# A linear-attention and dense kernel: the second block's loads go behind the boot's feature transfers, and some DMAs change their queue

## The chip, the cores and the metric

The kernel runs on one core of one Trainium2 chip. The time is that of the device in microseconds (us) for one execution. Before the change it is 690.11 us, the median of three runs (689.63 to 690.3).

The core has five engines that run side by side, each in the order of its own instructions: TensorE (PE: matmuls, and PEld: the loading of their weights), VectorE (DVE), ScalarE (ACT), GpSimd (POOL) and SyncE (SP, which only issues DMAs here). ScalarE and GpSimd issue DMAs too, each on a queue of its own.

## What is computed

```python
# r, k, v, w: (B, H, S, D) = (4, 8, 768, 48); u: (H, D)
for t in range(S):
    cur = einsum('bhd,bhe->bhde', u[None] * k[t], v[t])
    y[:, :, t] = einsum('bhd,bhde->bhe', r[t], state + cur)
    state = w[t][..., None] * state + einsum('bhd,bhe->bhde', k[t], v[t])
x = y.transpose(0, 2, 1, 3).reshape(3072, 384)
h = x @ w_in                    # w_in (384, 2048)
out = (h - tanh(h)) @ w_out     # w_out (2048, 384)
```

## The kernel before

**Blocks.** The 3072 tokens are eight blocks of 384 (two for each of the four sequences). For each block an attention part makes the features `xT` (384 features by 384 tokens), and a dense part takes them through 16 slices of 128 hidden units (`NF` = 16; the loop variable is `f`). While the dense part of block i runs, the attention of block i+1 is worked in between its steps. Only block 0 has its attention alone in front; this is called the boot.

**Attention of a block.** Inputs are the tiles `kq` (keys), `rp` (receptances), `wt` (decays), `v_sb`, and `rmix` and `kmix`, copies of r and k in which every second token is multiplied by `u` (the "mix"). Scores inside chunks of 64 tokens are built in levels m = 1, 2, 4, ... 32. Level 1 multiplies `kmix` and `rmix` on TensorE (`gram`, L219 to L237) and copies the wanted scores under a mask (L242). The later levels use `kq` and `rp` and after each of them both are multiplied by decays (`decay`, L267); products of decays come from `totals` (L253). After level 32 comes `turn` (transposes of `kq`, L317), `update` (matmuls at L335, states on VectorE at L345) and `result` (matmuls at L364 and L382, copies on ScalarE at L395 into `xT`, and into `late` for the last pair of heads). `late` is moved into the free rows of `xT` by six small DMAs (`fill_holes`, L402). These are the feature transfers, or fills; all six are issued by SyncE.

**Dense step f.** `first` makes three matmul pairs into `hp` (L476), six ScalarE activations (`h`, `s`, `qa`, `qb`, `th`, `big`, L483 to L488) and hands back five VectorE operations (L493 to L501) which are issued one step later. `Second.add` multiplies the slice by `w_out` into three accumulators (L514), three steps later (`LAG`); with the last slice ScalarE copies each accumulator to a tile `o` (L518) and issues its DMA to the output (L520).

**Weights.** They arrive as 16 tiles of 768 KB (`raw`) in a ring of three buffers. Each is turned into fp32 by two ScalarE activations (L165, L166) and three VectorE operations (L168, L169, L171). The first three loads are issued by SyncE, the others by GpSimd as buffers come free. Six tiles are converted in the boot, the other ten during block 0's dense steps 0 to 9 (their VectorE part one step later).

**Order.** Inside `manual_schedule(engines=...)` the named engines keep the order in which the program is written; the others are ordered by a scheduler with a cost model. In the boot only TensorE keeps the written order; in the loop TensorE, VectorE and ScalarE do. SyncE's DMA issues are placed by the scheduler everywhere. `plan(i)` says at which step f of block i's dense part each phase of block i+1's attention is put (`phases`), and at which step each preparation for a block is (`prep`: loads; `kmix`, `rmix`, the multiplication by `u`, L435; `totals`; `kq` and `rp`, the first decays). For i = 0 the levels start at step 3, otherwise at step 0. Input tiles have one buffer each, so a load for block i+2 waits until block i+1 has read the tile for the last time.

Of the kernel before, what the change touches and what calls it, by code (L numbers as in the profile page):

```python
# [37 lines left out]
F32 = mybir.dt.float32  # L38
# [4 lines left out]
AF = mybir.ActivationFunctionType  # L43
ALU = mybir.AluOpType
PSUM = bass.MemoryType.PSUM
PE, DVE, ACT = (getattr(mybir.EngineType, n) for n in ("PE", "DVE", "Activation"))

B, H, S, D = 4, 8, 768, 48
P = 128
# [12 lines left out]
NF = FF // P  # L62
N = B * S
# [20 lines left out]
def kernel(  # L84
# [10 lines left out]
    nc = tc.nc  # L95

    const = ctx.enter_context(tc.tile_pool(name="const", bufs=1))
# [10 lines left out]
    shift = const.tile([P, 3], F32, name="shift", tag="shift")  # L108
    for i, value in enumerate((QUAD[0][0], QUAD[1][0], -SMALL)):
        nc.vector.memset(shift[:, i:i + 1], value)  # L110
    u_sb = const.tile([P, NPAIR], F32, name="u_sb", tag="u_sb")
    nc.sync.dma_start(out=u_sb, in_=uT)

# [41 lines left out]
    def load_weights(f, queue):  # L155
        raw = conv.tile([P, 2 * DM, 2], I32, name="raw", tag="raw")
        queue.dma_start(out=raw, in_=weights[f].bitcast(I32).rearrange("p (n two) -> p n two", two=2))
        return f, raw

    def convert(f, raw):  # L160

        lo, hi = raw[:, :, 0], raw[:, :, 1]
        a = w_sb[:, f, :].bitcast(I32)
        up = conv.tile([P, 2 * DM], I32, name="up", tag="up", bufs=2)
        nc.scalar.activation(out=a.bitcast(F32), in_=hi.bitcast(F32), func=AF.Copy, scale=HIGH_SCALE)  # L165
        nc.scalar.activation(out=up, in_=lo.bitcast(U32), func=AF.Copy, scale=2.0 ** -29)  # L166
        return [
            lambda: nc.vector.tensor_single_scalar(a, a, 3, op=ALU.logical_shift_left),  # L168
            lambda: nc.vector.scalar_tensor_tensor(out=a, in0=hi, scalar=-2 ** 31, in1=a,  # L169
                                                   op0=ALU.bitwise_and, op1=ALU.bitwise_or),  # L170
            lambda: nc.vector.tensor_tensor(out=a, in0=a, in1=up, op=ALU.add)]  # L171
# [7 lines left out]
    class Block:  # L179
# [266 lines left out]
        def start(self, ps):  # L446

            for p0 in HALVES:
                for name, src in (("kq", kT), ("rp", rT), ("wt", wT)):
                    self.load(name, src, p0, UP)  # L450
            for name in ("rmix", "kmix"):
                self.tiles[name] = inp.tile([P, NPAIR * NB], F32, name=name, tag=name)
            yield
            for p0 in HALVES:
                self.mix(p0, UP)
                self.level_1(ps, p0)
                self.decay(1, p0, UP)
                self.totals(1, p0, UP)
            for m in (2, 4, 8, 16, 32):
                for p0 in HALVES:  # L460
                    self.level(ps, m, p0, UP)
                    self.totals(m, p0, UP)
            for p0 in HALVES:
                self.turn(ps, p0)
                self.update(ps, p0)
            for p0 in HALVES:
                self.result(ps, list(range(p0, p0 + UP)), p0 != HALVES[0])
                if p0 == HALVES[0]:
                    self.fill_holes([nc.sync])
            yield  # L470


# [30 lines left out]
    class Second:  # L503
# [5 lines left out]
        def add(self, f, g):  # L509
            if f == 0:  # L510
                self.acc = [self.ps.tile([P, DM], F32, name=f"acc{j}", tag=f"acc{j}", bufs=1)
                            for j in range(NB // P)]
            for j, acc in enumerate(self.acc):
                nc.tensor.matmul(acc, lhsT=g[:, j * P:(j + 1) * P], rhs=w_out_sb[:, f, :],  # L514
                                 start=(f == 0), stop=(f == NF - 1))
                if f == NF - 1:
                    o = dense.tile([P, DM], F32, name="o", tag="o")
                    nc.scalar.activation(out=o, in_=acc, func=AF.Copy, scale=1.0 / UPSCALE)  # L518
                    r0 = self.row0 + j * P
                    nc.scalar.dma_start(out=out[r0:r0 + P, :], in_=o)  # L520

    def plan(i):

        names = ("level 1", 2, 4, 8, 16, 32, "turn", "update")
        first_step = 3 if i == 0 else 0
        phases = {first_step + n: name for n, name in enumerate(names)}
        result = first_step + len(names) + 1
        phases[result] = "result"
        prep = {}

        def put(f, block, *what):
            prep.setdefault(f, []).extend((block, name) for name in what)

        if i == 0:
            put(0, 1, "kmix", "rmix")
            put(1, 1, "totals 1", "kq")
            put(2, 1, "totals 2", "rp")
        put(first_step + 1, i + 2, "load 1")
        put(first_step + 7, i + 2, "load 2")
        put(result + 1, i + 2, "load 3")  # L540
        for f, name in zip(range(NF - 6, NF), ("kmix", "rmix", "totals 1", "totals 2", "kq", "rp")):
            put(f, i + 2, name)
        return phases, prep

    blocks = [Block(b, q) for b in range(B) for q in range(NQ)]
    with tc.manual_schedule(engines={PE}), \
            tc.tile_pool(name="ps_boot", bufs=4, space=PSUM) as boot:
        xT = blocks[0].begin()
        start = blocks[0].start(boot)
        next(start)  # L550
        raws = [load_weights(0, nc.sync)]
        blocks[0].load_v()
        for f in range(1, RAWS):
            raws.append(load_weights(f, nc.sync))
        next(start)
        for f in range(AHEAD):
            for op in convert(*raws.pop(0)):
                op()
            raws.append(load_weights(f + RAWS, nc.gpsimd))
        for name in ("load 1", "load 2"):  # L560
            blocks[1].prepare(name)
    ps_d = ctx.enter_context(tc.tile_pool(name="ps_d", bufs=1, space=PSUM))
    ps_a = ctx.enter_context(tc.tile_pool(name="ps_a", bufs=2, space=PSUM))
    with tc.manual_schedule(engines={PE, DVE, ACT}):
        blocks[1].prepare("load 3")
        waiting, rest, extra = [], [], []
        for i, blk in enumerate(blocks):
            here = xT
            later = blocks[i + 1] if i + 1 < len(blocks) else None
            if later:  # L570
                xT = later.begin()
            phases, preparations = plan(i)
            second = Second(blk.b * S + blk.q * NB, ps_d)
            for f in range(NF):
                g, next_rest = first(here, f, ps_d)
                waiting.append((second, f, g))

                for n, op in enumerate(rest):
                    op()
                    if n >= 2 and extra:  # L580
                        extra.pop(0)()
                for op in extra:
                    op()
                rest = next_rest
                if later and f in phases:
                    later.phase(ps_a, phases[f])
                extra = convert(*raws.pop(0)) if raws else []
                for blk_p, name in preparations.get(f, ()):
                    if blk_p < len(blocks):
                        blocks[blk_p].prepare(name)  # L590
                if len(waiting) > LAG:
                    s, fs, gs = waiting.pop(0)
                    s.add(fs, gs)
                if i == 0 and f + AHEAD + RAWS < NF:
                    raws.append(load_weights(f + AHEAD + RAWS, nc.gpsimd))
        for op in rest:
            op()
        for s, fs, gs in waiting:
            s.add(fs, gs)
# [47 lines left out]
```

## Time and profile before

One execution was profiled. It took 690.1 us; its span, from the first to the last instruction, is 688.1 us (688.08 to the next digit), so 2.0 us lie around the span.

| engine | busy us | share of the span | instructions |
|---|---|---|---|
| PE (matmuls) | 648.3 | 94% | 8480 |
| PEld (weight loads) | 414.8 | 60% | 8480 |
| DVE | 567.4 | 82% | 1139 |
| ACT | 472.5 | 69% | 919 |
| POOL | 10.9 | 2% | 32 |

| DMAs | issued by | each | median us to landing |
|---|---|---|---|
| rmix, kmix, wt, kq, rp of a block | SyncE | 768 KB | 4.5 to 7.4 |
| v of a block | SyncE | 576 KB | 5.8 |
| weight tiles, 13 of 16 | GpSimd | 768 KB | 4.7 |
| fills `xT<-late`, 48 | SyncE | 24 KB | 2.7 |
| outputs, 24 | ScalarE | 192 KB | 1.8 |

Some times in the early part of the profile: block 0's inputs are issued from 1.27 us on; its level 1 matmuls start at 7.20; the scheduler issues block 1's rmix, kmix and wt at 11.85, 12.28 and 13.58, its kq at 35.89, and its rp and v at 45.69 and 46.31. The boot's last feature copy ends at 45.75, the first dense matmul starts at 47.46 and the first activation `h` at 52.38.

In lines of the timeline the first two numbers are the start and the duration in us, then engine, line, operation, and what it writes and reads; what stands in brackets is the idle time of the engine before, and what ended it. In lines of the chain of waits they are start and duration, then what the chain went through. "issue" is time in which the engine waited for nothing that the profile shows.

### The profile page before, as it was taken

The numbers are of one execution on the slowest core, as the hardware profiler recorded it, in microseconds if no ns is written. First come the engines' busy times: TensorE is split into PE (matmuls) and PEld (weight loads), VectorE is DVE, ScalarE is ACT, GpSimd is POOL, SyncE is SP. The second block draws the span as 40 slices with busy tenths as digits, with TensorE's granted clock in tenths as the row PEclk, the third lists the DMA queues.
The fourth block names the chain that finished last, engine by engine and source line by source line (L and its number), as shares of the span: only waits on it lengthen the run. The fifth ranks groups of instructions, "written<-read, shape, count | busy, mean of one in ns | idle before, by whom it ended". The sixth has DMA issues, their size and how long they took to land.

```text
span 688.1 us, 19930 instructions
## 1 busy us (share of the span) xinstructions
PE 648.3 (94%) x8480; PEld 414.8 (60%) x8480; DVE 567.4 (82%) x1139; ACT 472.5 (69%) x919; POOL 10.9 (2%) x32
## 2 busy tenths in 40 slices
PE   4766789999999999999999999999999999999997
PEld 3653455666665666666665666566665666655554
DVE  7788999999869897789879897698878898566764
ACT  3349578776768667776767667676768667788784
POOL 2010000000000000000000000000000000000000
PEclk9988899999999999999999999999999999999999
DMA  8376722241120401231130411223120010000000
GB/s 326 125 246 216 273 93 93 91 140 36 48 91 1 144 33 48 91 113 63 49 91 0 140 38 47 91 53 123 44 86 9 2 38 2 11 0 34 1 1 34
DMA packets 30840, 54.36 MB, mean 79 GB/s; under 512 B 2336, under 2 KB 28704, under 8 KB 30752
## 3 DMA queue, kind: packets, MB, share of 16 engines
q1 hardware_dynamic: 25424, 38.15, 17.1%
q0 software_dynamic: 1872, 10.22, 4.2%
q10 hardware_dynamic: 3456, 4.72, 1.8%
q8 instruction: 66, 1.08, 0.6%
q14 instruction: 22, 0.18, 0.1%
HBM read 47.19 MB, written 4.72 MB: 75 GB/s over the span
## 4 chain that ended last, share of the span: by engine, by line
PE 73%; DVE 12%; issue 5%; PEld 4%; ACT 3%; DMA 2%; SPq 1%; PEldq 1%; ACTq 0%; DVEq 0%
PE acc L514 31%; PE hp L476 29%; PE att L235 9%; DVE states L345 2%; PE att L382 2%; DVE w_sb L171 2%; PEld hp L476 2%; PE att L317 2%; PEld att L364 1%; DVE w_sb L169 1%; DVE hs L493 1%; PEld acc L514 1%; DVE rp L267 1%; DVE kq L267 1%; PE att L298 1%
## 5 line engine op out<-in xcount | busy, mean ns | idle before, releaser
L476 PE MATMUL hp<-xT,w_sb 128*128 128x384 f32 x768 | 273.1, 492 | 8.7 <-ACT h L483 5.2
L514 PE MATMUL acc<-w_sb,gT 128*128 128x384 f32 x768 | 277.7, 499 | 0.0
L476 PEld LDWEIGHTS hp<-xT,w_sb 128*128 128x128 f32 x768 | 147.0, 192 | 114.6 <-ACT h L483 8.4
L514 PEld LDWEIGHTS acc<-w_sb,gT 128*128 128x128 f32 x768 | 142.0, 192 | 90.0 <-issue 2.4
L483 ACT ACTIVATE h<-hp 128x384 f32<-128x384 f32 x128 | 62.8, 491 | 161.7 <-PE hp L476 157.9
L498 DVE TENSOR_TENSOR th<-h,th 128x384 f32<-128x384 f32 x128 | 71.1, 555 | 41.6 <-ACT th L487 41.5
L493 DVE SCALAR_TENSOR_TENSOR hs<-h,s 128x384 f32<-128x384 f32 x128 | 71.1, 556 | 21.3 <-ACT s L484 21.3
L501 DVE COPY_PREDICATED gT<-big,th 128x384 f32<-128x384 int32 x128 | 76.3, 596 | 12.9 <-ACT h L483 0.9
L485 ACT ACTIVATE qa<-s,shift 128x384 f32<-128x384 f32 x128 | 78.8, 615 | 4.2
L493 DVE SCALAR_TENSOR_TENSOR gT<-qb,hs 128x384 f32<-128x384 f32 x128 | 71.5, 558 | 9.3
L488 ACT ACTIVATE big<-s,shift 128x384 f32<-128x384 f32 x128 | 76.8, 600 | 0.0
L486 ACT ACTIVATE qb<-s,shift 128x384 f32<-128x384 f32 x128 | 76.7, 600 | 0.0
L235 PEld LDWEIGHTS att<-rp,kq 48*64 48x64 f32 x3072 | 55.0, 148 | 27.6 <-issue 16.7
L493 DVE SCALAR_TENSOR_TENSOR hs<-qa,hs 128x384 f32<-128x384 f32 x128 | 70.7, 552 | 0.0
L484 ACT ACTIVATE s<-h 128x384 f32<-128x384 f32 x128 | 67.0, 523 | 4.0
L235 PE MATMUL att<-rp,kq 48*64 48x32 f32 x3072 | 58.7, 231 | 11.5 <-DVE scores L242 4.9
L487 ACT ACTIVATE th<-h 128x384 f32<-128x384 f32 x128 | 64.9, 507 | 0.0
L267 DVE TENSOR_TENSOR kq<-kq,tot 128x768 f32<-128x768 f32 (+1 forms) x45 | 38.9, 864 | 11.5 <-PE att L235 11.5
L282 DVE COPY_PREDICATED scores<-mask_all,att 128x384 f32<-128x384 uint8 (+1 forms) x72 | 40.4, 622 | 0.0
L267 DVE TENSOR_TENSOR rp<-rp,tot 128x768 f32<-128x768 f32 (+1 forms) x45 | 38.9, 864 | 0.0
L345 DVE SCALAR_TENSOR_TENSOR states<-states,tot,att 128x48 f32<-128x48 f32 x176 | 31.6, 260 | 7.8 <-PE att L335 7.8
L235 PE MATMUL att<-rmix,kmix 48*64 48x64 f32 x768 | 14.5, 232 | 8.6 <-ACT rmix L216 7.2
(49 smaller groups left out, 343.8 us busy)
## 6 DMA issues: line engine op xcount, KB each, us to landing
raw<-in_weights POOLq DMA_DIRECT2D x13, 768.0 KB, 4.7
rmix<-in_rT SPq DMA_DIRECT2D x7, 768.0 KB, 4.6
kmix<-in_kT SPq DMA_DIRECT2D x7, 768.0 KB, 7.4
wt<-in_wT SPq DMA_DIRECT2D x7, 768.0 KB, 4.5
kq<-in_kT SPq DMA_DIRECT2D x7, 768.0 KB, 4.5
rp<-in_rT SPq DMA_DIRECT2D x7, 768.0 KB, 4.6
v_sb<-in_v SPq DMA_DIRECT2D x8, 576.0 KB, 5.8
out_y<-o ACTq DMA_DIRECT2D x24, 192.0 KB, 1.8
```

The lines of the kernel that those rows point to most:

```text
L235: nc.tensor.matmul(dst, lhsT=lhs[rows, t0:t0 + L], rhs=src, start=True, stop=True)
L267: nc.vector.tensor_tensor(out=part, in0=part, in1=by, op=ALU.mult)
L476: nc.tensor.matmul(hp, lhsT=w_in_sb[:, f, kc, :], rhs=xT[:, kc, :], start=(kc == 0), stop=(kc == KC - 1))
L484: nc.scalar.activation(out=s, in_=h, func=AF.Square)
L485: nc.scalar.activation(out=qa, in_=s, func=AF.Square, bias=shift[:, 0:1])
L486: nc.scalar.activation(out=qb, in_=s, func=AF.Square, bias=shift[:, 1:2])
L487: nc.scalar.activation(out=th, in_=h, func=AF.Tanh)
L488: nc.scalar.activation(out=big, in_=s, func=AF.Relu, bias=shift[:, 2:3])
L493: return lambda: nc.vector.scalar_tensor_tensor(out=out, in0=in0, scalar=scalar, in1=in1, op0=op0, op1=ALU.mult)
L498: lambda: nc.vector.tensor_tensor(out=th, in0=h, in1=th, op=ALU.subtract),
L501: lambda: nc.vector.copy_predicated(out=g, mask=big.bitcast(I32), data=th)]
L514: nc.tensor.matmul(acc, lhsT=g[:, j * P:(j + 1) * P], rhs=w_out_sb[:, f, :], start=(f == 0), stop=(f == NF - 1))
```

## The change

- Block 1's loads ("load 1" and "load 2") move from the end of the boot to the head of the loop, in front of "load 3", and SyncE is added to the engines that keep the written order, in the boot and in the loop. All six loads thus come behind the boot's fills on SyncE.
- The boot's six fills are issued by SyncE and ScalarE in turn, three each. Those of later blocks stay on SyncE.
- For block 0's dense part the levels start at step 4 instead of 3. Block 1's preparations move from steps 0, 1, 2 to steps 1, 2, 3, and its first decay of `rp` to step 4.
- For later blocks the first decay of `rp` moves from the last step of the dense part before to the step of level 1, behind it; the other preparations start at step 11 instead of 10.
- A one-column activation (Copy) is issued on ScalarE at the start, into a new tile `warm`.
- Outputs are issued by SyncE; only the very last one stays on ScalarE.

```diff
-PE, DVE, ACT = (getattr(mybir.EngineType, n) for n in ("PE", "DVE", "Activation"))
+PE, DVE, ACT, SP = (getattr(mybir.EngineType, n) for n in ("PE", "DVE", "Activation", "SP"))
...
+    warm = const.tile([P, 1], F32, name="warm", tag="warm")
+    nc.scalar.activation(out=warm, in_=shift[:, 0:1], func=AF.Copy)
...
                 if p0 == HALVES[0]:
-                    self.fill_holes([nc.sync])
+                    self.fill_holes([nc.sync, nc.scalar])
...
                     o = dense.tile([P, DM], F32, name="o", tag="o")
+                    rows = slice(self.row0 + j * P, self.row0 + j * P + P)
                     nc.scalar.activation(out=o, in_=acc, func=AF.Copy, scale=1.0 / UPSCALE)
-                    r0 = self.row0 + j * P
-                    nc.scalar.dma_start(out=out[r0:r0 + P, :], in_=o)
+                    queue = nc.scalar if rows.stop == N else nc.sync
+                    queue.dma_start(out=out[rows, :], in_=o)
...
-        first_step = 3 if i == 0 else 0
+        first_step = 4 if i == 0 else 0
...
         if i == 0:
-            put(0, 1, "kmix", "rmix")
-            put(1, 1, "totals 1", "kq")
-            put(2, 1, "totals 2", "rp")
+            put(1, 1, "kmix")
+            put(2, 1, "rmix", "totals 1")
+            put(3, 1, "totals 2", "kq")
+        put(first_step, i + 1, "rp")
         put(first_step + 1, i + 2, "load 1")
         put(first_step + 7, i + 2, "load 2")
         put(result + 1, i + 2, "load 3")
-        for f, name in zip(range(NF - 6, NF), ("kmix", "rmix", "totals 1", "totals 2", "kq", "rp")):
+        for f, name in zip(range(NF - 5, NF), ("kmix", "rmix", "totals 1", "totals 2", "kq")):
             put(f, i + 2, name)
...
-    with tc.manual_schedule(engines={PE}), \
-            tc.tile_pool(name="ps_boot", bufs=4, space=PSUM) as boot:
+    ctx.enter_context(tc.manual_schedule(engines={PE, SP}))
+    with tc.tile_pool(name="ps_boot", bufs=4, space=PSUM) as boot:
...
-        for name in ("load 1", "load 2"):
-            blocks[1].prepare(name)
...
-    with tc.manual_schedule(engines={PE, DVE, ACT}):
-        blocks[1].prepare("load 3")
+    with tc.manual_schedule(engines={DVE, ACT}):
+        for name in ("load 1", "load 2", "load 3"):
+            blocks[1].prepare(name)
```

## The prediction, made before the changed kernel was run

> **What bounds the kernel now.** I read the page's busy slices first, then busy time by stretches, then the chain of waits and the timeline of the early stretches, last the end. Slices of 17.2 us:
>
> ```profile
> PE   4766789999999999999999999999999999999997
> PEld 3653455666665666666665666566665666655554
> DVE  7788999999869897789879897698878898566764
> ```
>
> TensorE is full from the eighth slice on. The same by stretches (length; busy us and count of PE, PEld, DVE, ACT, POOL; granted TensorE clock, DMA share, GB/s):
>
> ```profile
> 12.00:23.00 11.00, 7.46 (x242) 7.01 (x236) 10.04 (x25) 4.35 (x5) 0.00 (x0) 1.00 1.00 379
> 45.00:54.00 9.00, 5.58 (x10) 2.31 (x11) 4.85 (x6) 4.04 (x7) 1.06 (x2) 0.62 0.96 341
> 54.00:66.00 12.00, 7.44 (x36) 3.60 (x38) 11.72 (x19) 11.87 (x22) 1.06 (x2) 0.86 0.62 225
> 106.00:124.00 18.00, 16.83 (x228) 10.98 (x228) 18.00 (x40) 16.26 (x30) 0.00 (x0) 1.00 0.21 70
> 124.00:688.00 564.00, 557.74 (x6814) 351.27 (x6812) 456.76 (x912) 397.92 (x789) 0.00 (x0) 1.00 0.17 55
> ```
>
> So three regimes. Up to 45 us the first block's attention runs alone; from 54 to about 112 VectorE is the bound (idle 0.28 us of 12, then none); from there TensorE is (idle 6.3 us in 564). The hand-over is the last wait of TensorE for VectorE, the second block's "turn" transpose:
>
> ```profile
> 112.23 0.98 PE L317 MATMUL att<-ident,kq 128*128 128x128 f32 x7 [1.17 <-DVE kq L267]
> ```
>
> What follows is 688.08 − 112.23 = 575.85 us of TensorE work which the change leaves as it is. The change can move only the time of that turn, the work still behind it, and the tail. Two losses before it matter. The chain of waits shows TensorE standing still while DMA is full (1.00 above, in the stretch 12 to 23):
>
> ```profile
> 21.07 2.45 issue
> ```
>
> It waits for no engine there, and starts again at 23.52, when the traffic ends: the same wait one batch of 127 matmuls later, with DMA at 15 GB/s, is 0.23 us. I read it as its instructions arriving late, behind data. The second loss is the feature fill, `late` into `xT`, which the first dense matmuls need:
>
> ```profile
> 41.31 0.49 ACT late L395
> ...
> 44.99 5.55 DMA xT<-late
> 50.54 0.14 issue
> 50.68 1.62 PE hp L476 x2
> ```
>
> VectorE uses part of this time for the second block's two mixes, and is idle for 3.95 us of the rest:
>
> ```profile
> 45.73 0.95 DVE L435 TENSOR_TENSOR kmix<-kmix,u_sb 128x768 f32<-128x768 f32 x1
> ...
> 48.48 0.95 DVE L435 TENSOR_TENSOR rmix<-rmix,u_sb 128x768 f32<-128x768 f32 x1
> ...
> 54.25 0.56 DVE L168 TENSOR_SCALAR w_sb<-w_sb 128x768 int32<-128x768 int32 x1 [3.95 <-ACT w_sb L165]
> ```
>
> **The change, part by part.** The sum is made on the profiled run: span 688.08 us, 690.1 us in all, so 2.0 us lie around the span; the median of the runs is 690.11.
>
> *Loads of block 1 leave the boot (−2.2).* rmix, kmix and wt (768 KB each) were issued at 11.85, 12.28 and 13.58 and landed 8.7 to 11.7 us later; the earlier loads (2.36 MB of features, three weight tiles of 0.79, v of 0.59: 5.3 MB) at the measured 288 and 379 GB/s would be through at about 17. The stall at 21.07 then loses its cause and shrinks to 0.23. VectorE waits 2.36 us at 24.85 for the matmuls behind that stall, so it gains as much: −2.2, everything after it 2.2 earlier. Bounds: 0 if it is no DMA effect, −3.4 if the 1.23 us of "issue" at 15.71 goes too; I keep that one, since 5.3 MB still run beside it.
>
> *Fill on two queues (−1.8).* SyncE issues six fills 0.63 apart, 41.82 to 45.58. Three on each queue end their issue 1.9 sooner (the last at 43.09 instead of 44.99); with the same 5.55 to land, 48.64 instead of 50.54. ScalarE pays three issues (0.34 for an output's, 0.59 for a fill's: 1.0 to 1.8) in front of an idle 1.05 and the four xT copies that end at 45.75, so these end by 46.5. In old times the first four matmuls could start at 46.5 instead of 47.46; at the granted 0.50 of this spot they take 2.9, the last two 1.6: done at 51.0 instead of 52.3, −1.3. All this lies 2.2 earlier, where the clock was still 1.00 for about 1.2 us: −2.4. I take −1.8 between them. Bounds 0 (fills land later behind other traffic) and −3.6 (all six in 2.2, as at 63.56). The first `h` comes at 52.38 − 4.0 = 48.4.
>
> *Block 1's mixes move into the dense steps (+1.74).* 0.87 each start to start, formerly in VectorE's idle time, now (steps 1 and 2) in the stretch that VectorE bounds. Bounds 0 (it finds idle time there, as ScalarE is nearly full too: 11.87 of 12) and +1.74. totals, kq and rp only change places inside that stretch.
>
> *Levels one step later (+0.65).* One more dense step precedes the turn. On VectorE it costs 5 products and 3 conversion steps: 64.22 to 68.77, 4.55. TensorE in turn has one pair less behind the turn: 1.94 + 1.94, 3.9. Net +0.65, bounds 0 and +0.8.
>
> *Loads late? (0).* In the new order SyncE issues the six (4.52 MB) from 41.82 − 2.2 + 3 × 0.63 = 41.5. rp and v, issued at 45.69 and 46.31 beside weights, moved 1.38 MB until 59.1: 103 GB/s, the low bound. The high one: 341 GB/s less one weight tile per 5 us, 184. VectorE wants kmix at 61.88 − 4.0 = 57.9 (where totals 1 began), wt after rmix one step on (63.3), kq at 71.2, rp at 78.5. At 184 kmix lands at 50.0 and wt at 54.3; at 103 at 56.8 and 64.4, kq at 72.0, rp at 79.7. That is 0 to +1.2; I take 0, as most weight tiles need only part of each 5 us.
>
> A rule that speaks against this part: the Trainium skill, "DMA: Bandwidth & Descriptors", section "Queues, rings and completion order", says that each DMA engine takes turns between its queues, one packet each. On the page the software queue's packets average 5.5 KB and SyncE's 1.5 KB; taken by turns, an estimate from the rule gives SyncE 21% while weights are in flight, some 81 GB/s, and by it the sum would end near 699 if weights never paused. The row of 103 GB/s includes pauses, and decides here.
>
> *Dummy activation (0).* The one table load sits at 4.68 to 5.96, ahead of block 0's first mix. VectorE waits until 7.21 for wt, and has no idle time from there to the level 1 scores at 10.27, whose matmuls ended at 8.76: earlier mixes are covered. The second half waits for its own DMA (ScalarE at 8.54 and 9.56). Without that cover at most −1.3; +0.1 for one more instruction.
>
> *rp of the later blocks at step 0 (0).* 0.87 on VectorE after the level 1 scores, six times. Around 146 the scores start at 147.89 and would let rp end near 150.6; level 2's matmuls come at 151.59. Covered by 1.0; without it +0.9 per block, 5 in all.
>
> *Outputs by SyncE (−0.5).* They wait there for ScalarE's copies at step 2; behind them on SyncE stands kq of step 7, due at step 15. ScalarE loses 24 issues that matter only at the end:
>
> ```profile
> 683.65 0.49 ACT L518 ACTIVATE o<-acc 128x384 f32<-128x384 f32 x1 [0.47 <-PE acc L514]
> 684.17 0.34 ACTq L520 DMA_DIRECT2D out_y<-o  x1
> 684.62 0.49 ACT L518 ACTIVATE o<-acc 128x384 f32<-128x384 f32 x1 [0.47 <-ACT o L518]
> ```
>
> The last copy waits for the issue of the one before, not for matmuls (over at 683.94): it can start at 684.1. Bounds 0 and −0.6.
>
> Sum: −2.2 − 1.8 + 1.74 + 0.65 − 0.5 = −2.1: span 686.0, time **688.0 us**.
>
> **The rivals.** *Nothing to be measured* (0.2% of 690.11 is 1.4 us, about what a measurement of this kernel tells from no change). The fill gains nothing because three queues now compete: −2.1 + 1.8 = −0.3, 689.8. For it: the six fills took 4.7 us to land beside weights alone, against 2.7 over all blocks. Against: those issued earlier land earlier. *More gain.* VectorE has idle time in steps 0 and 1, which swallows the mixes, and the fill is at full clock: −2.1 − 1.74 − 1.8 = −5.6, 684.5. For it: the 3.95 us of idle were a wait for ScalarE. Against: 11.72 busy of 12 afterwards. *Slower: block 1's loads come late.* VectorE works in order, so dense work stands behind kmix, and TensorE behind that. At 90 GB/s kmix is 1.0 late, wt 3.4 more, kq 0.8, rp 1.5: +6.7, 694.7. It outweighs the gain below about 100 GB/s. For it: rp and v had 103 beside the same weight tiles. Against: both had landed by 59.1, though issued behind the fills. That the loads do not move is excluded by the order of SyncE's instructions, now written out.
>
> **How the numbers follow.** Forecast 0.45; no difference 0.22; more gain 0.2; late loads 0.13. Chances: faster 0.64, same 0.22, slower 0.14 (the last takes a little of what the forecast's own range, 686.3 to 689.6, leaves). The range: 684.6, where "more gain" sits, to 692.0, the sum with a fill that gains nothing, a fetch that keeps its 2.2 and nothing else lost; beyond it lie most of the late loads and the extreme of more gain, some 2 in 10.
>
> **What would show it.** Right: no "issue" stall above 0.5 at 21 us; DMA near 0 from 17 to 33; first `h` near 48.4; no VectorE wait for kmix, wt, kq or rp; the turn near 112.23 + 4.55 + 1.74 − 4.0 = 114.5, and 575.85 − 3.9 − 0.5 = 571.4 from it to the end. Wrong: VectorE waiting for a load between 55 and 80; a first `h` after 50.5; a TensorE wait before level 2 of a later block; or a new order of VectorE's boot work, which the scheduler still chooses.

## The result, and the profile after

The changed kernel took 690.72 us in the median (690.06 to 692.98), the kernel before, run beside it, 689.87 (689.35 to 690.84): a ratio of 1.0019 with a 95% interval from 1.0001 to 1.0037. Measured again on another occasion it took 690.50 (689.67 to 692.57) against 690.4, ratio 1.0007 [0.9998, 1.0015]. So the change gains nothing; 688.0 had been forecast. The profiled execution is its fastest: 690.06, span 687.7, while the one profiled before stands near its median.

First the page's busy slices, then the same stretches as before (length; busy time and count of PE, PEld, DVE, ACT, POOL; granted TensorE clock, DMA share, GB/s):

```profile
PE   3877799999999999999999999999999999999997
...
DVE  7879999989869997699878997599977998576664
```

```profile
12.00:23.00 11.00, 9.14 (x316) 8.80 (x308) 10.00 (x24) 4.32 (x5) 0.00 (x0) 1.00 0.46 178
23.00:31.00 8.00, 6.57 (x208) 5.58 (x203) 7.96 (x26) 2.78 (x9) 0.00 (x0) 1.00 0.02 5
...
45.00:54.00 9.00, 8.15 (x12) 3.09 (x12) 5.17 (x8) 5.18 (x8) 1.06 (x2) 0.52 1.03 387
54.00:66.00 12.00, 7.63 (x12) 3.76 (x13) 11.86 (x19) 11.80 (x22) 1.58 (x3) 0.62 1.04 392
```

The three regimes are the same as before. In the stretch 12 to 23 the traffic fell from 379 to 178 GB/s and TensorE's busy time rose from 7.46 to 9.14: that part of the change works. The traffic stands now from 45 to 66, at 387 and 392 GB/s where there were 341 and 225, and there TensorE has half its clock (0.52 and 0.62, before 0.62 and 0.86).

TensorE's timeline shows that the stall at 21.07 is gone, since matmuls run from 18.15 to 26.2 as one line, but that the one ahead of it stays, 1.78 (1.23 before), behind a stretch with 407 GB/s (14 to 16.37; 6 GB/s from 18.15 to 21); the third line is the turn:

```profile
15.72 0.65 PE L238 MATMUL att<-rp,kq 48*64 48x32 f32 x13
18.15 8.08 PE L238 MATMUL att<-rp,kq 48*64 48x32 f32 x253 [1.78 <-issue]
...
116.37 1.53 PE L320 MATMUL att<-ident,kq 128*128 128x128 f32 x12 [1.09 <-DVE kq L270]
```

The turn comes 4.14 later than before (112.23), where 2.3 had been forecast. ScalarE's timeline shows a wait that was not there before. Its order is `h`, `s`, the converts of the boot's sixth weight tile (`w_sb`, `up`), then `qa`:

```profile
40.00 0.48 ACT L398 COPY late<-att 128x384 f32<-128x384 f32 x1 [0.18 <-PE att L385]
40.51 2.21 ACTq L405 DMA_DIRECT2D xT<-late  x3
...
49.10 0.49 ACT L486 ACTIVATE h<-hp 128x384 f32<-128x384 f32 x1 [0.68 <-PE hp L479]
49.62 0.52 ACT L487 ACTIVATE s<-h 128x384 f32<-128x384 f32 x1
52.15 0.89 ACT L168 ACTIVATE w_sb<-raw 128x768 f32<-128x768 f32 x1 [2.00 <-DMA raw<-in_weights]
52.95 0.89 ACT L169 ACTIVATE up<-raw 128x768 int32<-128x768 uint32 x1
53.75 0.60 ACT L488 ACTIVATE qa<-s,shift 128x384 f32<-128x384 f32 x1
...
57.27 0.46 ACT L486 ACTIVATE h<-hp 128x384 f32<-128x384 f32 x1
```

Before, `h` stood at 52.38, the convert at 53.33 without a wait, `qa` at 54.93 and the second `h` at 58.46. The first `h` is 3.28 earlier now, `qa` and the second `h` only 1.2. The chain that ended last goes through the weight tile too, not through the fills. It comes to it from VectorE, whose conversions free the buffer that the tile is loaded into, and shows after it the half clock: six matmuls of a step in 4.22, in 1.94 a little later:

```profile
37.04 2.19 DVE states L348 x12
39.23 0.87 DVE w_sb L174
...
43.71 8.41 DMA raw<-in_weights
52.15 0.89 ACT w_sb L168
...
57.78 4.22 PE hp L479 x6
...
69.01 1.94 PE hp L479 x6
```

With these lines the difference between the two profiled executions can be booked by stretches; times of before and after, from the timelines. Its sum is -0.4, as the change's is its fastest; the medians differ by +0.85 and +0.1.

| stretch | before | after | measured | forecast |
|---|---|---|---|---|
| start to first `h` | 52.38 | 49.10 | -3.28 | -4.0 |
| first to second `h` | 6.08 | 8.17 | +2.09 | 0 |
| second `h` to block 1's turn | 53.77 | 59.10 | +5.33 | +6.29 |
| that turn to the next block's (178.91; 179.92) | 66.68 | 63.55 | -3.13 | -3.9 |
| from there to the last turn (572.00; 573.03) | 393.09 | 393.11 | 0 | 0 |
| last turn to the last `o` (684.62; 684.19) | 112.62 | 111.16 | -1.46 | -0.5 |
| rest of the span | 3.5 | 3.5 | 0 | 0 |
| sum | | | -0.4 | -2.1 |

### The profile page after: what moved, and what is told of

Read it like the earlier page. It is cut to its first block, busy times and chain, and to the rows that moved or that the text cites. A ratio compares the mean times of both kernels' runs of the same rounds, so it can differ in the third digit from the quotient of the medians.

```text
span 687.7 us, 19941 instructions
## 1 busy us (share of the span) xinstructions
PE 651.3 (95%) x8480; PEld 416.2 (61%) x8480; DVE 568.3 (83%) x1139; ACT 471.6 (69%) x920; POOL 10.9 (2%) x32
## 4 chain that ended last, share of the span: by engine, by line
PE 77%; DVE 8%; PEld 4%; issue 4%; ACT 3%; DMA 2%; PEldq 0%; SPq 0%; DVEq 0%
PE acc L517 32%; PE hp L479 31%; PE att L238 9%; DVE states L348 2%; PEld hp L479 2%; PE att L320 2%; PE att L385 2%; PEld att L367 1%; DMA raw<-in_weights 1%; PEld acc L517 1%; DVE w_sb L174 1%; DMA rp<-in_rT 1%; DVE w_sb L172 1%; PE att L338 1%; PE att L301 1%
## 5 line engine op out<-in xcount | busy, mean ns | idle before, releaser
L479 PE MATMUL hp<-xT,w_sb 128*128 128x384 f32 x768 | 277.1, 498 | 8.2 <-ACT h L486 5.2
L479 PEld LDWEIGHTS hp<-xT,w_sb 128*128 128x128 f32 x768 | 148.8, 195 | 116.1 <-ACT h L486 8.6
```

The lines of the kernel that those rows point to most:

```text
L479: nc.tensor.matmul(hp, lhsT=w_in_sb[:, f, kc, :], rhs=xT[:, kc, :], start=(kc == 0), stop=(kc == KC - 1))
```

## The experiments

Each was timed against the kernel before on the same chip (690.2 to 690.5 in the median); experiments from different chips are compared by these ratios. The change itself stands at 1.0007 in this scale, and 0.1% is 0.69 us.

**The change once more**, unaltered.

> The changed kernel once more. In its profile the boot's last weight tile landed 8.4 us after its issue and ScalarE waited 2.0 us for it, and kmix landed at 58.1, 1.6 us before VectorE wanted it. Theory 'contention' (the six loads behind the fills share the DMA with the weight tiles, and late arrivals eat the gain): times spread over some 3 us, and in a slow run VectorE waits for kmix or ScalarE longer for the weight tile; median near 690.7. Rival 'plan' (the levels one step later and the mixes in VectorE's full stretch cost 2.4 us, the loads are harmless): also near 690.7, but with no wait for a load in the profile, and the spread comes from the start.

690.50, ratio 1.0007 [0.9998, 1.0015]. In its profile the first `h` is at 48.32, ScalarE waits 1.82 for the sixth weight tile, the second `h` is at 56.78 and the turn at 115.87. No wait of VectorE for a load of block 1. The wait comes again, and its size moves with the landing of the tile. The chain that ended last goes through the seventh tile here (issued at 45.91, 9.24 to its landing).

**Block 1's loads back in the boot**, the rest as in the change.

```diff
-    ctx.enter_context(tc.manual_schedule(engines={PE, SP}))
-    with tc.tile_pool(name="ps_boot", bufs=4, space=PSUM) as boot:
+    with tc.manual_schedule(engines={PE}), \
+            tc.tile_pool(name="ps_boot", bufs=4, space=PSUM) as boot:
...
+        for name in ("load 1", "load 2"):
+            blocks[1].prepare(name)
...
-    with tc.manual_schedule(engines={DVE, ACT}):
-        for name in ("load 1", "load 2", "load 3"):
-            blocks[1].prepare(name)
+    with tc.manual_schedule(engines={PE, DVE, ACT}):
+        blocks[1].prepare("load 3")
```

SyncE's order goes back to the scheduler with it.

> The changed kernel with block 1's loads back in the boot, placed by the scheduler as before the change; new plan, two fill queues, dummy activation and outputs by SyncE stay. Contention: the stall of 2.45 us at 21 us comes back (+1.3 to +2.2), the weight tiles are on time (-1 to -2): 690.0 to 691.5, no wait of ScalarE for a weight tile after the first h. Plan: nothing is won by the weight tiles: 692 to 693.

692.00, ratio 1.0029 [1.0018, 1.0040]. TensorE's timeline has the stall back:

```profile
17.06 4.13 PE L238 MATMUL att<-rp,kq 48*64 48x32 f32 x126 [1.78 <-issue]
23.64 4.35 PE L238 MATMUL att<-rp,kq 48*64 48x32 f32 x133 [2.46 <-issue]
```

So the stall belongs to the loads, and moving them is worth 0.22%, 1.5 us. ScalarE still waits 1.99 for the sixth weight tile, against the first of the two expectations: the wait needs neither rmix, kmix, wt nor kq behind the fills. rp and v still stand there (issued at 43.68 and 44.29).

**The steps of before with the late loads.**

```diff
-        first_step = 4 if i == 0 else 0
+        first_step = 3 if i == 0 else 0
...
-            put(1, 1, "kmix")
-            put(2, 1, "rmix", "totals 1")
-            put(3, 1, "totals 2", "kq")
-        put(first_step, i + 1, "rp")
+            put(0, 1, "kmix", "rmix")
+            put(1, 1, "totals 1", "kq")
+            put(2, 1, "totals 2", "rp")
...
-        for f, name in zip(range(NF - 5, NF), ("kmix", "rmix", "totals 1", "totals 2", "kq")):
+        for f, name in zip(range(NF - 6, NF), ("kmix", "rmix", "totals 1", "totals 2", "kq", "rp")):
```

> The changed kernel with the steps as before the change (levels from step 3, kmix and rmix at step 0, totals 1 and kq at step 1, totals 2 and rp at steps 2 and 15). Contention: VectorE comes to kmix near 54 and waits until it lands (58.1 in the changed kernel), then for wt (61.6) and kq (66.2): 3 to 6 us of waits against 2.4 won by the plan, 691.5 to 694.5. Plan: 2.4 won, little waiting: 688.3.

693.56, ratio 1.0044 [1.0032, 1.0056]. Here the load is late; the table of waits (total, times, longest):

```profile
PE att L238 <- DVE scores L245: 8.0, 1, 8.0
DVE kmix L438 <- DMA kmix<-in_kT: 4.6, 1, 4.6
```

The late loads don't go with the old steps, so the later steps are part of their price.

**The fill on one queue again**, the rest as in the change.

```diff
-                    self.fill_holes([nc.sync, nc.scalar])
+                    self.fill_holes([nc.sync])
```

> The changed kernel with all six fills issued by SyncE. The fills' issue ends 1.9 us later and so the six loads start 1.9 us later. Both theories: the first h comes 1 to 2 us later. Contention: the weight tile of the boot is less disturbed (-1), kmix is later (60.0, just at VectorE's need): 690.5 to 692. Plan: +1.8, 692.5.

690.91, ratio 1.0010 [0.9999, 1.0021]: the second queue is worth 0.2 here, within the interval of nothing. The first `h` is 1.0 later than in the change (50.09), but ScalarE takes the weight tile at 51.04 without a wait, and `qa` comes at 52.63, earlier than the change's 53.75. The second `h` is at 57.48 all the same (57.27 in the change): ScalarE waits 1.23 for the seventh tile instead.

**No dummy, and all outputs by ScalarE.**

```diff
-    warm = const.tile([P, 1], F32, name="warm", tag="warm")
-    nc.scalar.activation(out=warm, in_=shift[:, 0:1], func=AF.Copy)
...
-                    queue = nc.scalar if rows.stop == N else nc.sync
+                    queue = nc.scalar
```

> The changed kernel without the dummy activation and with all outputs issued by ScalarE. Both theories: the tail is 0.5 us longer, the dummy activation is worth nothing, as VectorE waits for wt until 7.1 or later: +0.5, 691.0, the stretch from the turn to the end 571.9 instead of 571.4.

691.96, ratio 1.0024 [1.0010, 1.0038]: 1.2 slower than the change, more than the 0.5 forecast for these two parts. The two were then undone singly, below.

**Five weight tiles in the boot instead of six**, the rest as in the change.

```diff
-AHEAD = 6
+AHEAD = 5
```

> The changed kernel with AHEAD = 5: the boot converts five weight tiles, the sixth is converted as an extra of step 0, so ScalarE meets it behind the six activations of step 0 and not between s and qa. Theory 'weight tile' (the earlier first h only runs into ScalarE's in-order wait for the boot's sixth weight tile, which lands 7.5 to 8.4 us after its issue): ScalarE's second h comes 2 to 3 us earlier (54 to 55 instead of 57.3), the turn 1 to 2 us earlier, 688.5 to 689.5. Rival 'VectorE' (VectorE has the same work anyway and bounds the stretch): the second h is earlier, the turn is not, 690.5.

688.98, ratio 0.9979 [0.9970, 0.9989]. The second `h` comes at 54.45. VectorE waits 1.6 for `kmix` in this profile, the slowest of its executions: dense steps that come earlier meet the end of the late loads' slack.

**Loads in the gap, steps of before.** The chip's DMA is idle from 23 to 31. SyncE is made to wait for it: a transfer of 96 bytes reads a total that level 16 writes, and rmix, kmix and wt are queued behind it; kq stands behind the turns, rp and v behind the fills. The rest (fill, dummy, outputs) is as in the change.

```diff
+    gate = const.tile([1, 24], F32, name="gate", tag="gate")
...
+                    if m == 16 and p0 == HALVES[0]:
+                        nc.sync.dma_start(out=gate, in_=self.tots[32, p0][0:1, 0:24])
+                        blocks[1].prepare("load 1")
...
+            blocks[1].prepare("load 2")
```

> The changed kernel with block 1's rmix, kmix and wt issued by SyncE when level 16 of the boot is through (a 96-byte DMA that reads a total holds them back), kq behind the boot's turns, rp and v behind the fills; and the steps as before the change. DMA is nearly idle from 23 to 34, so the loads should meet neither the boot's second instruction batch nor the weight tiles of 41 to 52, and the mixes stand at step 0 in VectorE's idle time. Theory 'weight tile': turn 1.3 (fetch) plus 0.5 to 1.5 earlier than the 112.2 of before: 687 to 688.5. Rival 'start-up spread' (early gains are lost in the spread of the first loads): 689.5 to 690.5.

688.44, ratio 0.9970 [0.9961, 0.9980]. The DMA issues of 10 to 40 us (KB each, us to landing) show the loads at their usual speed:

```profile
rmix<-in_rT SPq DMA_DIRECT2D x1, 768.0 KB, 4.6
kmix<-in_kT SPq DMA_DIRECT2D x1, 768.0 KB, 7.6
wt<-in_wT SPq DMA_DIRECT2D x1, 768.0 KB, 8.5
```

In the change the same three took:

```profile
rmix<-in_rT SPq DMA_DIRECT2D x1, 768.0 KB, 9.9
kmix<-in_kT SPq DMA_DIRECT2D x1, 768.0 KB, 15.0
wt<-in_wT SPq DMA_DIRECT2D x1, 768.0 KB, 17.9
```

With the loads in the gap the mixes stay in VectorE's idle time and the old steps hold.

**Loads in the gap, the change's steps.** As the one before, with the change's plan: the diff of the steps above, the other way round.

> The same place of the loads, with the changed kernel's steps. It tells the plan's own price, free of late loads: one more step in front of the turn (4.55 against a pair of 3.9) and the two mixes in VectorE's full stretch (1.74): 2.4 us more than the run with the old steps, 689.5 to 691. If the price is only nominal (VectorE has idle time in steps 0 and 1): the same as the run with the old steps, within 0.7.

691.20, ratio 1.0009 [0.9999, 1.0020]. The plan alone costs 0.39%, 2.7 us; the sum had 2.39 for it (1.74 + 0.65).

**Loads in the gap, steps of before, five weight tiles.** The gap version with `AHEAD = 5`.

> e5_gap_old_plan with the boot converting five weight tiles instead of six. Theory (the boot's sixth weight tile is what ScalarE waits for between s and qa of step 0, and it costs about 1.5 whichever way block 1's loads are queued): the 1.5 that e7_five_tiles measured add to the 2.0 of e5_gap_old_plan, 686.5 to 687.3, ScalarE's wait for raw ahead of qa(0) gone, and the second h two to three ahead of e5's. Rival (the gap's loads already have SP's transfers out of the way, so the tile is late for another reason, or the converts come due later): 688.0 to 689.0, no change from e5.

685.54 (683.14 to 686.36), ratio 0.9926 [0.9911, 0.9940]: faster than both kernels. ScalarE's timeline goes from `h` to `qa` without a weight tile between:

```profile
50.11 0.49 ACT L491 ACTIVATE h<-hp 128x384 f32<-128x384 f32 x1 [1.81 <-PE hp L484]
50.63 0.52 ACT L492 ACTIVATE s<-h 128x384 f32<-128x384 f32 x1
51.19 0.61 ACT L493 ACTIVATE qa<-s,shift 128x384 f32<-128x384 f32 x1
...
54.72 0.47 ACT L491 ACTIVATE h<-hp 128x384 f32<-128x384 f32 x1
```

From `h` to `h` 4.61 instead of the change's 8.17; the turn is at 107.58.

**The kernel before with five weight tiles**, nothing else.

> The kernel before with five weight tiles in its boot and nothing else changed. Theory (before, the sixth tile was there in time: no wait for raw in its profile, and qa(0) followed h at 2.55; the wait is new in the change, because the fills end earlier): nothing gained, 689.8 to 690.8 against 690.4, and the second h within 0.5 of 58.46. Rival (the tile and its convert stand in ScalarE's way before as well, so the 1.5 of e7_five_tiles are worth the same without the change): 688.5 to 689.3.

688.40, ratio 0.9973 [0.9962, 0.9984]: the rival held. The sixth tile costs the kernel before as much as the change: 0.27% there and 0.28% here (0.9979 against 1.0007), 1.9 us each. Even without a wait its two converts stand between `s` and `qa`, 1.6 of ScalarE's time. So the gain from five tiles does not measure the new wait; the wait has to be read from the profiles. Nor does taking the tile away give the forecast gain back: with five tiles the change (0.9979) is no faster than the kernel before (0.9973), and in its profile the wait of 1.6 for `kmix` has taken the place.

**No dummy alone**, and **all outputs by ScalarE alone**; each is one half of the double edit above.

> The change without the dummy activation; outputs by SyncE as in the change. e4_no_warm_outputs_act lost 1.5 against the change, of which 0.5 were expected from the outputs. Theory A (the dummy hides the table load, which lies ahead of kmix at 4.68 without it, but the first matmul waits for weights from VectorE or for wt later than that): as the change, 690.2 to 691.0. Theory B (the table load of 1.28 comes back onto the path of the first level): 691.5 to 692.3, with TensorE's first level about 1 later than 6.3 to 7.2.

690.06, ratio 0.9994 [0.9985, 1.0003]. Nothing is lost without the dummy; by the ratios 0.9 is gained, and 1.1 in the other pair that differs by it alone, the double edit (1.0024) and the next run (1.0040). Each is about as large as its uncertainty.

> The change with the dummy kept and all outputs queued by ScalarE, as before. Theory A (ScalarE's four DMA issues at the end of each block cost only at the end of the last block, where three o copies are 0.96 apart instead of 0.64): 690.9 to 691.3, the time from the last turn's place to the end 0.5 above the change's 571.4 to 572.3. Theory B (the issues hold up ScalarE in all blocks and TensorE waits for its results): 691.7 to 692.5, the time from turn to end 2 above, spread over the eight blocks.

693.13, ratio 1.0040 [1.0025, 1.0055], 2.3 slower than the change. Its profile has 112.60 from the last turn to the last `o`, as before, and 111.16 is what every version with SyncE's outputs shows. By the last `o` this profile is 4.1 behind the change's. 1.4 of that stands ahead of the turn (117.76), where a weight tile landed late (ScalarE waits 2.99); the outputs can't have caused this, as the first of them comes 100 us later. 1.4 stands behind the last turn, and 1.3 between the turns, with no cause shown.

**The kernel before with SyncE's outputs alone.**

```diff
-                    nc.scalar.dma_start(out=out[r0:r0 + P, :], in_=o)
+                    queue = nc.scalar if r0 + P == N else nc.sync
+                    queue.dma_start(out=out[r0:r0 + P, :], in_=o)
```

> The kernel before with one part of the change: outputs queued by SyncE, except the last. The prediction's term: 0.5, from the last three o copies alone (0.96 apart, 0.64 after): 690.0. Theory from the profiles (from the last turn at 572.00 to the last o copy it is 112.62 before and 111.16 in the change, in every profile with ScalarE's issues 112.60 and in every one with SyncE's 111.16; where the last block begins, ScalarE's three copies and issues keep TensorE's acc at 2.60 instead of 2.10): 1.4, 688.9 to 689.3.

689.15, ratio 0.9983 [0.9974, 0.9992]: 1.2 gained, 0.6 to 1.8, against a term of 0.5. The missing part is where the last block begins. ScalarE's timeline of the kernel before:

```profile
628.14 0.47 ACT L518 ACTIVATE o<-acc 128x384 f32<-128x384 f32 x1
628.64 0.34 ACTq L520 DMA_DIRECT2D out_y<-o  x1
629.02 0.49 ACT L518 ACTIVATE o<-acc 128x384 f32<-128x384 f32 x1 [0.42 <-PE hp L476]
...
630.89 0.49 ACT L483 ACTIVATE h<-hp 128x384 f32<-128x384 f32 x1 [0.47 <-PE acc L514]
```

and of the change:

```profile
629.17 1.22 ACT L522 ACTIVATE o<-acc 128x384 f32<-128x384 f32 x3
630.28 0.49 ACT L486 ACTIVATE h<-hp 128x384 f32<-128x384 f32 x1
```

From the first copy to the next `h` it is 2.75 before and 1.11 after. TensorE's two groups of step matmuls around it start 4.58 apart before (626.85, 631.43) and 3.87 after (627.88, 631.75): 0.71 which the prediction didn't see, beside the 0.64 of the last three copies, for which it had 0.5.

**The kernel before with its fills on two queues**, nothing else. The edit is the line above the other way round, in two places: in the boot and in `phase`. So the fills of later blocks are split as well, three issues of each block on ScalarE, which the change does not do.

> The kernel before with one part of the change: the boot's fills on two queues. The prediction's term: 1.8, 688.7, first h at 50.6, second at 56.7. Theory (SyncE's next loads then start 2 us earlier and share the transfers with the boot's sixth weight tile, which lands at 52.0 to 52.6 instead of 50.3, so ScalarE waits behind s and only 0.5 to 0.8 of the 1.8 pass on to the second h): 689.6 to 690.0, first h at 50.6, a wait for raw of 1 to 2 behind s, second h at 57.7 to 58.0.

689.80, ratio 0.9998 [0.9989, 1.0007]: 0.1 gained, between -0.5 and 0.8, against a term of 1.8. The later blocks' fills may hide some gain: from the first turn to the last `o` its profile has 573.32, 0.9 more than before. So the boot's part alone is measured by undoing it in the change, above. This profile, of the slowest execution, shows the new wait with none of the other parts present. TensorE's and ScalarE's timelines:

```profile
48.62 4.18 PE L476 MATMUL hp<-xT,w_sb 128*128 128x384 f32 x6 [3.94 <-DMA xT<-late]
...
52.90 0.49 ACT L483 ACTIVATE h<-hp 128x384 f32<-128x384 f32 x1 [2.87 <-PE hp L476]
53.42 0.52 ACT L484 ACTIVATE s<-h 128x384 f32<-128x384 f32 x1
56.02 0.89 ACT L165 ACTIVATE w_sb<-raw 128x768 f32<-128x768 f32 x1 [2.08 <-DMA raw<-in_weights]
```

Here the first `h` doesn't come earlier: 10.9 behind the `late` copy (42.02), 11.1 in the kernel before. TensorE's first matmul waits for the fills until 48.62, and its six take 4.18 behind that. In the kernel before the first four start while fills are still on their way:

```profile
47.46 2.90 PE L476 MATMUL hp<-xT,w_sb 128*128 128x384 f32 x4 [3.08 <-DMA xT<-late]
50.68 1.60 PE L476 MATMUL hp<-xT,w_sb 128*128 128x384 f32 x2 [0.33 <-DMA xT<-late]
```

**The gap version with four weight tiles**, `AHEAD = 4`.

> e8_gap_old_plan_five with four weight tiles in the boot. Theory A (a tile's converts in the boot's end stand in ScalarE's way each time, about 1.5): 683.8 to 684.8. Theory B (only the sixth stands between s and qa of step 0; the fifth is converted while ScalarE waits for hp, and with four the step's own converts come one step later under the same waits): 685.0 to 686.5, as with five. Theory C (a tile then comes too late for its step): slower than 686.5 with a TensorE wait for w_sb.

686.66, ratio 0.9949 [0.9936, 0.9961]. Not better than five. In its profile `late` is at 41.73 and the first `h` at 50.74, with five 40.26 and 50.11. So no gain from a second tile less is seen; what stands in its way is not traced.

## Why the prediction was wrong, step by step

- **Loads leave the boot (forecast -2.2).** The mechanism is right: the stall at 21 is gone, and undoing the move brings its 2.46 back. The size is 1.5 when undone. `late` came 1.3 earlier instead of 2.2, as block 0's wt let VectorE start at 8.17 instead of 7.21 and the first stall grew from 1.23 to 1.78. The start lies anywhere between 6.9 and 8.8 over the profiles, without the dummy at 7.22 and 8.78, so no run ties its shift to the change.
- **Fill on two queues (forecast -1.8): the step that failed.** Undone alone in the change, the part is worth 0.2, give or take about 1.0. "The first `h` comes at 52.38 − 4.0 = 48.4" was nearly so (49.10, 48.32 in the second profile). That everything behind it moves by the same was not. Behind `s`, in ScalarE's order, stand the converts of the boot's sixth weight tile. With the fill on one queue that tile landed 6.1, 6.2 and 6.6 us after its issue (three profiles); with two queues 7.4 to 11.1 (ten). ScalarE waits 1.8 to 3.0 for it in five of these, 0.25 and 0.32 in two, and not at all in three where the first `h` came after 50.4. So `qa` gains 1.2 where `h` gains 3.3.

  Over all profiles the fill shows no gain at `qa`: from the `late` copy to `qa` it is 12.6 to 13.6 in the three profiles with one queue, 12.6 to 15.6 in the ten with two. What the step had wrong is the path behind `h`: the sum took the tile as given, because it had shown no wait before: 3.0 of slack (landed at 50.4, used at 53.33). Its user was to come 4.0 earlier; the tile was issued only 0.45 earlier (43.71, before 44.16) and took 2.2 longer. That it takes longer because SyncE's next loads follow the shorter fills sooner (42.48 in the change, 44.35 with the fill on one queue) fits the full DMA of that stretch, but no run held those loads back alone: it is argued, not shown.

  In the three two-queue profiles with VectorE's old boot order (next point) even the first `h` gained nothing: 10.9 to 11.2 behind `late`, 10.6 to 11.1 with one queue in that order.
- **Dummy (forecast 0): a term that the sum had at nothing.** It saved nothing, as said, but with it the scheduler ordered VectorE's boot work anew: "a new order of VectorE's boot work", which the prediction lists as a sign of being wrong. One operation of a weight conversion stood in front of the second half's states in the kernel before, and stands behind them in the change (39.23 in the chain above). What follows the states then comes 0.87 later. The order before:

```profile
36.56 0.95 DVE L171 CUSTOM_DVE_ANT_0 w_sb<-w_sb,up 128x1536 uint16<-128x1536 uint16 x1
38.35 2.19 DVE L345 SCALAR_TENSOR_TENSOR states<-states,tot,att 128x48 f32<-128x48 f32 x12 [0.84 <-PE att L335]
```

  The sixth tile is issued 5.81 after these states begin in all six profiles without the dummy and 6.7 to 6.8 after in all eleven with it. So up to 0.87 of ScalarE's wait comes from there, and the price of the dummy may be the 0.9 and 1.1 of its two pairs.
- **The plan (forecast +2.4).** 2.7 by the pair of gap versions. In the table its two parts are +5.33 and -3.13 instead of +6.29 and -3.9. Of the 0.77 that the second is short, 0.43 is a stall ("issue") in the middle of block 1's matmuls with the scores; the rest is not traced. The stall is there, 0.43 to 1.06 long, in all nine profiles with the change's steps, and at that place in none of the eight with the old ones. The prediction had no term for it:

```profile
132.94 1.45 PE L385 MATMUL att<-scores,v_sb 64*48 64x64 f32 x85
134.81 0.42 PE L385 MATMUL att<-scores,v_sb 64*48 64x64 f32 x11 [0.43 <-issue]
```

- **Outputs by SyncE (forecast -0.5).** Mis-sized: 1.46 in the profile, 1.2 alone. The step looked at the kernel's last copies only; ScalarE's issues bind a second time where the last block begins, with no preparation on TensorE to cover them. This error hid the one above: turn to end came out at 571.3, forecast 571.4, from two that cancel.
- **Loads late (forecast 0).** Right. kmix was used at 59.75, 1.6 after it landed, wt, kq and rp with more. rmix to v, 4.52 MB, were in flight from 42.48 to 71.7: 155 GB/s, between the bounds of 103 and 184. The Trainium skill ("DMA: Bandwidth & Descriptors", "Queues, rings and completion order") led to an estimate of 81 GB/s by turns of one packet, if weights never paused. Here they did not pause, as each tile issued from 43.71 to 71.34 was issued before the one ahead of it had landed, and the measured 155 decides.
- **rp at step 0 (forecast 0).** Right: no wait of TensorE for VectorE between that turn and the next.

By single parts, in us from the ratios: loads -1.5, fill -0.2, plan +2.7, outputs -1.2, dummy +0.9, together +0.7; measured +0.5 [-0.1, +1.0] in the second timing. Each is uncertain by about 1, so that the sum closes is no proof. The rival "nothing to be measured" was the nearest (689.8), and its reason held: the fill gains nothing. It put the cause on the fills themselves. That is seen where the first `h` gained nothing; in the change's profiles the first `h` did come earlier, and what was late was the next thing in ScalarE's order.

A rule fits here that the prediction did not weigh: the Trainium skill, "DMA: Bandwidth & Descriptors", section "Issuing engines are not separate DMA queues", says that starting transfers from several engines saves only the time of issuing, as the same 16 DMA engines carry them all. The runs agree: the six issues took 2.2 in all instead of 3.8, and of the 1.6 saved 0.2, within the interval of nothing, reached the end. ScalarE's three took 2.21, above the 1.0 to 1.8 of the prediction.

## What to carry to other kernels

When a wait ends earlier, follow the in-order queue of the engine that waited: the next item with a DMA behind it needs slack of the full gain, or the gain ends there. Loads put beside a full DMA took about twice as long here, so look for a stretch in which DMA is idle and queue the loads behind something that ends at its start: with the loads in the gap, the old plan and the other parts of the change the gain was 0.3%, and with the sixth weight tile taken out of the boot 0.74% (outputs by SyncE alone gave 0.17%, five tiles alone 0.27%). An edit on one engine can change the order that a scheduler picks on another: compare the order, not the edited line alone. Look for an issue's cost at every place where the bound engine loses its cover, not at the end alone.

## What had not been expected of the hardware

- The same three loads of 768 KB, queued one behind the other, took 9.9, 15.0 and 17.9 us to land beside weight tiles, at 387 to 392 GB/s in all, and 4.6, 7.6 and 8.5 in an idle stretch.
- TensorE stands with no wait that the profile shows ("issue") in the boot, about 127 matmuls apart, when traffic has run ahead: 2.45 after 382 GB/s (16.94 to 21.07, before), 1.78 after 407 GB/s (change), and 0.17 or nothing in the change with 5 to 6 GB/s (18.15 to 26.4). That its instructions arrive late is a reading of this; no run shows them.
- In the change the granted clock was 0.52 and 0.62 from 45 to 66, and four groups of six step matmuls in a row ran at half speed (4.22 against 1.94), where before two such groups did: part of an earlier start is lost there. The Trainium skill ("TensorE: Matmul & The Clock Gate", "What's actually happening") has the clock throttled by default until activity releases it. The rows show the throttled clock; TensorE counts as busy for 8.15 of 9 us there, so they don't show what releases it.
- The executions of the change spread over about 3 us (690.06 to 692.98). The kernel before spread over 1.5 beside it, but over 2.3 to 3.0 in the sets of 19 to 33 beside the experiments, so the spread is no mark of the change. Two landings vary by as much: block 0's wt (VectorE starts at 6.9 to 8.8) and the sixth weight tile (7.4 to 11.1 us). That they make the spread is an inference; few executions were profiled.
